# Two K loads ranked higher in a load queue, and another table of rankings, in a kernel of two attentions

## The chip, the core and the metric

The kernel runs on one core of a Trainium2 chip. A core has five engines that run their own instruction streams and meet at semaphores: TensorE (PE; matmul, with weight loads shown as PEld), VectorE (DVE), ScalarE (ACT), GpSimd (POOL) and SyncE (SP). Here SP issues all loads. Matmul results go to PSUM, eight banks of 128 x 2 KB; everything else lies in SBUF. The metric is device time in microseconds of one execution, the median of several runs.

## What is computed

Two attention blocks on different inputs; their outputs stand side by side. A has 32 query heads on 4 K/V heads (eight query heads share one), B has 32 query heads with 32 K/V heads of their own. Both have 16 batches of 32 tokens, width 1024, 1024 cached keys, heads of 128, all bf16.

```python
def _B_ref(x, k_cache, v_cache, wq, wo):
    B, Sq, D = x.shape              # 16, 32, 1024
    H, Dh = 32, 128
    q = (x @ wq).reshape(B, Sq, H, Dh).transpose(0, 2, 1, 3)
    scores = einsum("bhqd,bhkd->bhqk", q, k_cache) * (Dh ** -0.5)
    p = softmax(scores, axis=-1)
    o = einsum("bhqk,bhkd->bhqd", p, v_cache)
    return o.transpose(0, 2, 1, 3).reshape(B, Sq, H * Dh) @ wo
# _A_ref: the same with 4 heads of k_cache and v_cache, each repeated 8 times
# returned: concatenate([a, b], axis=-1)
```

B's cache is 16 x 32 x 1024 x 128 x 2 bytes for K and as much for V, 268 MB of the 338 MB that are read.

## The kernel before

**Units of work.** A is cut into 128 quads: one batch, four query heads, all 1024 keys. B is cut into 64 pairs, 0 to 63 in the program's order, each of two batches and four heads; a pair has four tiles of K (512 KB each, loaded two at a time) and four loads of V (512 KB each). For a pair of B the steps are:

- the load of K by SP (`st_dmaKB`, L904), two loads `y = 2n` and `y = 2n + 1` for pair `n`; each brings two tiles
- four transposes in place on VectorE (`st_ktrB`, L973, 128 x 1024 as f32 units)
- the scores on TensorE (`st_scoresB`, L1030, 64 small matmuls into four PSUM banks)
- two maxima on VectorE (`st_max`, L1045), the exponentials on ScalarE (`st_exp`, L1061; they free the banks), sums and exchange between lanes on GpSimd and ScalarE (`st_weights`, L1077 to L1088)
- scaling of the probabilities on GpSimd (`st_pscale`, L1161; from pair `NORM_FROM` = 61 on the outputs are scaled instead, `st_normB`, L1175 and L1176, on ScalarE or VectorE)
- two transposes on TensorE (`st_ptB`, L1132), each evacuated from PSUM (`evac`, L650), the products with V (`st_pvB`, L1149), evacuation, a small transpose (`st_otrB`, L1187), evacuation
- after every two pairs the output projection of their group of tokens (`oproj`, L817) and its addition on VectorE (L829, L838; for the very last group L833, then the store, L835)

The steps of a quad of A are alike (scores L992, maximum L1042, exponential L1054, scaling L1280, transposes L1099, products L1119, transposes of K on TensorE L966).

**Buffers.** K of B has eight tile slots in `KB_sb`, and late in the kernel four more in `wq_sb`; pair 61's K stands in slots 0 to 3 of `KB_sb`, pair 62's in slots 4 to 7, pair 63's in `wq_sb`. The V of pair 63 is loaded into slots 0 to 3 of `KB_sb` (`home_v`), once pair 61's scores have been made.

**Who sets the order.** The program is first recorded as a list of 5431 operations with their dependences, and each gets a step number. `list_schedule` then plans: it keeps a time for every engine and for the DMA stream, takes the engine that can start first, and among the operations that can start within a small look-ahead it takes the one of the highest rank. The outcome is one fixed order for each engine. On the chip each engine runs its list strictly in that order, and waits at semaphores; SP too, so a load whose slot is not free yet holds all loads behind it. An evacuation marked `any` is given to ScalarE or VectorE by the planner.

A rank is made as follows (L278). For a step before `tail_step` (120, 122 or 124) it is `bl`, the length of the path behind the operation within its step, and `step_us` (2.5 to 5) is taken off for every step number. For later steps it is the full length of the path to the end, less a base. `RANKS` holds 16 such rules. `TUNE` is a table of 71 entries: after every 77 planned operations the planner goes on to the next entry, which names the rule that holds from there. So a change of an entry changes the plan from its place on, until the two plans fall together again. The operation's own `prio` is part of `bl`, and is 0 for all here. Loads of K get a step number two or so pairs ahead of their use: loads 124 and 125, pair 62's, have step 120; loads 122 and 123, pair 61's, have 118; loads 126 and 127, pair 63's, have 122.

Of the kernel before, what the change touches and what calls it, by code (L numbers as in the profile page):

```python
# [17 lines left out]
XT_FREE = 54  # L18
LATE = 51
NORM_FROM = 61  # L20
NKB_SLOTS = 8
LAZY_PER_STEP = 100
LAZY_DELAY = 4
# [21 lines left out]
RANKS = ((3.5, 122, 0.35, 0.0, 0.3), (3.0, 122, 0.35, 0.0, 0.3), (4.0, 122, 0.35, 0.0, 0.3), (3.5, 122, 0.15, 0.0, 0.3), (2.5, 122, 0.35, 0.0, 0.3), (5.0, 122, 0.35, 0.0, 0.3),  # L45
         (3.5, 122, 0.7, 0.0, 0.3), (3.5, 120, 0.35, 0.0, 0.3), (3.0, 124, 0.2, 0.0, 0.3), (3.5, 122, 0.15, 1.5, 0.3), (3.5, 122, 0.15, -1.5, 0.3), (3.5, 122, 0.15, 0.0, 0.0),
         (3.5, 122, 0.15, 0.0, 0.7), (3.5, 122, 0.15, 4.0, 0.3), (3.5, 122, 0.15, -4.0, 0.3), (3.5, 122, 0.25, 0.0, 0.3))
TUNE = (11, 11, 6, 10, 15, 6, 8, 15, 12, 2, 7, 0, 11, 12, 9, 12, 5, 6, 0, 7, 0, 7,
        4, 4, 8, 8, 1, 1, 7, 15, 0, 7, 7, 7, 0, 0, 0, 7, 1, 2, 0, 0, 7, 0,
        3, 0, 2, 11, 15, 11, 15, 5, 3, 0, 1, 3, 6, 15, 8, 13, 3, 3, 0, 13, 10, 3,  # L50
        9, 9, 9, 3, 1)
HOLD_AHEAD = 1
STEP_NEAR = 0
TAIL_BASE = 12.0
# [76 lines left out]
class Prog:  # L131
# [118 lines left out]
    def list_schedule(self, lat=0.05, look=LOOK):  # L250
        ops = self.ops
        n = len(ops)
# [11 lines left out]
        bl = [0.0] * n  # L264
# [7 lines left out]
        full = [0.0] * n  # L272
        for i in range(n - 1, -1, -1):
            full[i] = odur(ops[i]) + max((full[u] + lat for u in users[i]), default=0.0)
        ranks = []
        for step_us, tail_step, _, bias, _ in RANKS:
            base = max((full[i] for i in range(n) if ops[i].step >= tail_step and ops[i].dma_key is None), default=0.0)
            ranks.append([(bl[i] if ops[i].step < tail_step else full[i] - base + TAIL_BASE) - step_us * min(ops[i].step, tail_step) + (bias if ops[i].first else 0.0) for i in range(n)])  # L278
        bl = ranks[0]
        ready_t = [0.0] * n  # L280
        free = {}
# [139 lines left out]
        while True:  # L421
            best = None
            bkey = None
            turn = len(order) // WINDOW
            turn = TUNE[turn] if turn < len(TUNE) else 0
            bl, look, act_first = ranks[turn], RANKS[turn][2], RANKS[turn][4]
# [70 lines left out]
        for k in seq:  # L497
            eng, emit, reads, writes, dma_key, name, dur, tag, prio = self.specs[order[k]]
# [55 lines left out]
def build(nc, pa, pb, out):  # L554
# [6 lines left out]
    Dh = pa["k"].shape[3]  # L561
    Sk = pa["k"].shape[2]
# [7 lines left out]
    NVB = NVB_SLOTS  # L570
    NKB = NKB_SLOTS
    HqA = pa["wq"].shape[1] // Dh
# [16 lines left out]
    with stack:  # L589
# [305 lines left out]
        def st_dmaKB(y):  # L895
            if y < NIT:
                kind, sl = home_k(2 * y)
                assert home_k(2 * y + 1) == (kind, sl + 1) and sl % 2 == 0
                q = quadsB[2 * (y // 2)]
                dst = (wq_sb if kind == "wq" else KB_sb)  # L900
                dst = dst[:, 2 * sl:2 * sl + 4, :].rearrange("p j c -> p (j c)") if kind == "wq" else dst[:, sl:sl + 2, :].rearrange("p i x -> p (i x)")
                src = pb["k"][q.b0 + y % 2, q.m * MS:(q.m + 1) * MS].rearrange("h (p s) d -> (h p) (s d)", s=32)
                pr.step, was = 2 * ((2 * y - NKB) // 4) if 2 * y >= NKB else pr.step, pr.step
                pr.add("sp", lambda e: e.dma_start(dst, src), writes=[(kind, sl), (kind, sl + 1)], dma_key=f"{kind.lower()}{sl}", name="kb_dma",  # L904
                       dur=4 * Sk * Dh * 2, wtag={(kind, sl): 2 * y, (kind, sl + 1): 2 * y + 1})
                pr.step = was

        V_LAST = 2 * NIT - 4
# [17 lines left out]
        def home_k(x):  # L926
            if x < XK:
                return ("KB", x % NKB)
            return ("wq", (x - XK) % (NKB + 4)) if (x - XK) % (NKB + 4) < 4 else ("KB", kb_of(x))
# [226 lines left out]
        def st_pscale(q):  # L1156
            def emit(e):
                for h_ in range(2):
                    k_ = 20 + 2 * q.e + h_
                    p_ = p2_of(q.vP)[:, h_ * 512:(h_ + 1) * 512]  # L1160
                    last = e.tensor_scalar(p_, p_, stat2[:, q.vB.idx, k_:k_ + 1], 1.0, ALU.mult, ALU.mult)  # L1161
                return last
            pr.add("pool", emit, reads=[q.vB], writes=[q.vP], name="pscaleB")

        def st_copyB(vbo, h_, vO):
            evac(lambda: O2_sb[:, vO.idx, :, :, :].rearrange("p i u d -> p (i u d)"), lambda: bank(vbo[h_]), reads=[], writes=[vbo[h_], vO], name="O_ev")
# [49 lines left out]
        def pairB(n):  # L1216
# [3 lines left out]
            if n == 0:  # L1220
                for y in range(2, NKB // 2):
                    st_dmaKB(y)
            st_scoresB(qs)
            while k_next[0] < min(NIT, 2 * n + 2 + NKB // 2 + (2 if n >= LATE else 0)):
                st_dmaKB(k_next[0])
                k_next[0] += 1
# [9 lines left out]
            for q in qs:  # L1236
                if n < NORM_FROM:
                    st_pscale(q)
# [16 lines left out]
            for h_ in range(2):  # L1255
                vO = Virt("O2")
                if n < NORM_FROM:
                    st_copyB(vbo, h_, vO)
# [36 lines left out]
        for y in range(2):  # L1295
            st_dmaKB(y)
# [122 lines left out]
```

## Time and profile before

| | us |
|---|---|
| median of 3 runs | 857.17 |
| lowest and highest | 856.28, 862.17 |
| the profiled execution | 854.25 |
| its span, first to last instruction | 852.5 |

The granted TensorE clock was 0.996 over the execution. In the profile "PE x13382" counts instructions, digits are busy tenths of a slice of 1/40 of the span (21.3 us), and a row of the order of time gives start, duration, engine, line, operation and operands; the name in brackets is what ended the idle time before it. "issue" stands for idle time without a wait that the profile shows. A DMA row with "SPq" is the time at which SP issued the load; when it landed is told by the median from issue to landing.

SP's own waits are longest for the slots of V, which products with V free (L1149), 217.0 us in 84 waits; for slots of K (freed by scores, L1030) it waits 77.3 us in 31. While SP waits the DMA engines work off what was issued before.

### The profile page before, as it was taken

What the parts mean: (1) busy time and instruction counts of PE and PEld (TensorE: products, weight loads), DVE (VectorE), ACT (ScalarE), POOL (GpSimd) and SP (SyncE); (2) the same over time, 40 slices, a digit from 0 to 9 for tenths busy, and PEclk for the clock granted to TensorE, in tenths of its full rate; (3) what the DMA queues carried; (4) which work ended last, traced back from release to release, by engine and by line L of the source; (5) the groups of instructions that cost most, each with busy time, mean ns of one, the idle gap of its engine ahead of it and who ended that gap; (6) DMA issues with size and microseconds to landing.
All of it is one profiled execution on the core that took longest, in us unless ns stands there. A gap on an engine that the chain in (4) does not pass through costs nothing.

```text
span 852.5 us, 31891 instructions
## 1 busy us (share of the span) xinstructions
PE 762.9 (89%) x13382; PEld 518.7 (61%) x13504; DVE 746.7 (88%) x960; ACT 590.9 (69%) x1458; POOL 461.9 (54%) x1160
## 2 busy tenths in 40 slices
PE   6988999989889889999998998999998898878887
PEld 5455666666566566666666656566666656555655
DVE  1598879979899888898999888899989899999986
ACT  2377777687777576777667767686677677686754
POOL 1056565646456454564655555555664645655852
PEclk9989999999999999999999999999999999999999
DMA  9999999999999999999999999999999999999993
GB/s 354 415 396 417 414 413 420 403 415 405 389 411 406 420 414 415 371 397 416 418 418 415 418 397 415 401 407 414 417 420 414 410 417 393 410 419 405 403 400 139
DMA packets 93791, 341.83 MB, mean 401 GB/s; under 512 B 10000, under 2 KB 10256, under 8 KB 77264
## 3 DMA queue, kind: packets, MB, share of 16 engines
q1 hardware_dynamic: 93088, 337.94, 98.7%
q8 instruction: 107, 1.75, 0.7%
q0 software_dynamic: 560, 1.84, 0.5%
q14 instruction: 36, 0.29, 0.1%
HBM read 337.64 MB, written 2.10 MB: 399 GB/s over the span
## 4 chain that ended last, share of the span: by engine, by line
PE 51%; DVE 21%; ACT 11%; DMA 7%; POOL 5%; issue 3%; SPq 1%; DVEq 0%; POOLq 0%; ACTq 0%
PE psum L1149 9%; PE psum L817 9%; DVE KB_sb L973 6%; DVE stat L1045 6%; PE psum L1030 6%; PE psum L1099 5%; DMA KB_sb<-in_B_k_cache_dram 5%; PE psum L1119 4%; PE psum L734 4%; ACT P_sb L1054 4%; DVE stat L1042 4%; PE psum L1132 4%; ACT P_sb L1061 4%; PE psum L774 4%; PE psum L992 3%
## 5 line engine op out<-in xcount | busy, mean ns | idle before, releaser
L973 DVE STREAM_TRANSPOSE KB_sb<-KB_sb 128x1024 f32<-128x1024 f32 x240 | 284.7, 1218 | 10.9 <-DMA KB_sb<-in_B_k_cache_dram 10.5
L1161 POOL TENSOR_SCALAR P_sb<-P_sb,stat 128x512 bf16<-128x512 bf16 x232 | 158.3, 695 | 92.7 <-DVE stat L1088 63.7
L1280 POOL TENSOR_SCALAR P_sb<-P_sb,stat 128x1024 bf16<-128x1024 bf16 x128 | 143.6, 1122 | 87.6 <-DVE stat L1196 70.1
L1077 POOL COPY stat<-stat 32x4 f32<-32x4 f32 x512 | 92.5, 181 | 173.1 <-DVE stat L1045 102.2
L1061 ACT ACTIVATE P_sb<-psum,stat 128x512 bf16<-128x512 f32 x236 | 159.4, 690 | 33.5 <-DVE stat L1045 29.1
L1054 ACT ACTIVATE P_sb<-psum,stat 128x1024 bf16<-128x1024 f32 x128 | 143.4, 1121 | 42.3 <-DVE stat L1042 41.9
L1045 DVE TENSOR_REDUCE stat<-psum 128x2 f32<-128x1024 f32 x128 | 150.2, 1211 | 23.6 <-PE psum L1030 23.0
L1042 DVE TENSOR_REDUCE stat<-psum 128x1 f32<-128x1024 f32 x128 | 153.4, 1204 | 6.6 <-PE psum L992 5.7
L650 ACT COPY PT_sb<-psum 128x512 f32<-128x512 f32 x174 | 101.5, 590 | 53.7 <-PE psum L1132 32.0
L1149 PE MATMUL psum<-VB_sb,PT_sb 64*64 64x256 bf16 x3584 | 115.2, 272 | 8.7 <-issue 2.0
L1149 PEld LDWEIGHTS psum<-VB_sb,PT_sb 64*64 64x64 bf16 x3584 | 92.4, 107 | 29.6 <-issue 21.6
L1099 PE MATMUL psum<-id,P_sb 128*128 128x128 f32 x512 | 90.3, 300 | 12.1 <-POOL P_sb L1280 3.3
L1099 PEld LDWEIGHTS psum<-id,P_sb 128*128 128x128 f32 x512 | 73.6, 208 | 33.7 <-POOL P_sb L1280 11.1
L1132 PE MATMUL psum<-id,P_sb 128*128 128x128 f32 x472 | 81.3, 300 | 11.2 <-POOL stat L1077 4.6
L1119 PE MATMUL psum<-PT_sb,VA_sb 128*128 128x128 bf16 x1024 | 79.8, 220 | 8.8 <-ACT P_sb L1054 3.6
L1132 PEld LDWEIGHTS psum<-id,P_sb 128*128 128x128 f32 x472 | 67.2, 209 | 31.3 <-POOL P_sb L1161 13.7
L1119 PEld LDWEIGHTS psum<-PT_sb,VA_sb 128*128 128x128 bf16 x1024 | 63.0, 96 | 33.9 <-issue 12.5
L1030 PE MATMUL psum<-KB_sb,QR 32*32 32x512 bf16 x3840 | 73.6, 397 | 9.0 <-ACT P_sb L1054 5.6
L650 ACT CAST O_sb<-psum 128x512 bf16<-128x512 f32 x96 | 54.2, 591 | 25.3 <-PE psum L1149 25.2
L992 PE MATMUL psum<-KTA_sb,QT_sb 128*128 128x512 bf16 x189 | 63.4, 380 | 8.1 <-ACT P_sb L1061 2.5
L817 PE MATMUL psum<-woB_sb,OTB_sb 128*128 128x512 bf16 x231 | 61.0, 379 | 6.6 <-ACT P_sb L1061 1.6
L774 PE MATMUL psum<-xT_sb,wq_sb 128*32 128x512 bf16 (+1 forms) x1024 | 64.6, 375 | 0.9 <-issue 0.9
(80 smaller groups left out, 987.9 us busy)
## 6 DMA issues: line engine op xcount, KB each, us to landing
KB_sb<-in_B_k_cache_dram SPq DMA_DIRECT2D x120, 1024.0 KB, 9.5
VB_sb<-in_B_v_cache_dram SPq DMA_DIRECT2D x234, 512.0 KB, 8.2
KA_sb<-in_A_k_cache_dram SPq DMA_DIRECT2D x64, 256.0 KB, 7.6
VA_sb<-in_A_v_cache_dram SPq DMA_DIRECT2D x64, 256.0 KB, 7.6
wq_sb<-in_B_wq_dram SPq DMA_DIRECT2D x16, 512.0 KB, 9.7
woB_sb<-in_B_wo_dram SPq DMA_DIRECT2D x32, 256.0 KB, 8.7
woA_sb<-in_A_wo_dram SPq DMA_DIRECT2D x32, 256.0 KB, 7.9
wq_sb<-in_B_k_cache_dram SPq DMA_DIRECT2D x8, 1024.0 KB, 8.4
```

What stands on the lines that cost most here:

```text
L650: return e.copy(dst, src) if hasattr(e, "activation") else e.tensor_copy(dst, src)
L973: pr.add("dve", lambda e: e.transpose(tile_k(x).bitcast(F32), tile_k(x).bitcast(F32)), writes=[home_k(x)], name="KBt_tr", rtag={home_k(x): ...
L1042: pr.add("dve", lambda e: e.tensor_reduce(stat[:, vst.idx, 0:1], both(vS), AXIS.XY, ALU.max, negate=True), writes=vS + [vst], name="max")
L1045: pr.add("dve", lambda e: e.tensor_reduce(stat2[:, q.vB.idx, 2 * q.e:2 * q.e + 2], both(vS), AXIS.X, ALU.max, negate=True), writes=vS + [q ...
L1054: return e.activation(dst, src, ACTF.Exp, bias=stat[:, vst.idx, 0:1], scale=1.0, accum_out=stat[:, vst.idx, 1:2])
L1061: last = e.activation(dst, src, ACTF.Exp, bias=stat2[:, q.vB.idx, k_:k_ + 1], scale=1.0, accum_out=stat2[:, q.vB.idx, 4 + k_:5 + k_])
L1099: last = e.transpose(bank(vb)[:, m * P:(m + 1) * P], p32[:, m:Sk // 2:NPK], id32[:])
L1119: last = e.matmul(bank(vb)[:, 0:P], VA_sb[:, kvs, c, :], ptc_of(vPT, c, 0, P), start=(c == 0), stop=(c == NCH - 1))
L1132: last = e.transpose(bank(vb)[:, m * P:(m + 1) * P], p32[:, m:Sk // 2:4], id32[:])
L1149: last = e.matmul(bank(vbo[h_])[n0:n0 + 64, i * 2 * Dh:(i + 1) * 2 * Dh], pt2_chunk(vPT, c, e0, n0), v2[e0:e0 + 64, c * 2 * Dh:(c + 1) * 2 ...
L1161: last = e.tensor_scalar(p_, p_, stat2[:, q.vB.idx, k_:k_ + 1], 1.0, ALU.mult, ALU.mult)
L1280: pr.add("pool", lambda g: g.tensor_scalar(P_sb[:, vP.idx, :], P_sb[:, vP.idx, :], stat[:, vst.idx, 2:3], 1.0, ALU.mult, ALU.mult), reads= ...
```

## The change

Two loads get a `prio` of 30 us: `KPRIO` names loads 124 and 125, both halves of the K of pair 62. The value enters `bl`, and by an added term also the rank of the late steps. 26 of the 71 entries of `TUNE` change, from the eighth on; the other 45 keep the rule that they had.

```diff
+KPRIO = {124: 30.0, 125: 30.0}
...
-TUNE = (11, 11, 6, 10, 15, 6, 8, 15, 12, 2, 7, 0, 11, 12, 9, 12, 5, 6, 0, 7, 0, 7,
-        4, 4, 8, 8, 1, 1, 7, 15, 0, 7, 7, 7, 0, 0, 0, 7, 1, 2, 0, 0, 7, 0,
-        3, 0, 2, 11, 15, 11, 15, 5, 3, 0, 1, 3, 6, 15, 8, 13, 3, 3, 0, 13, 10, 3,
-        9, 9, 9, 3, 1)
+TUNE = (11, 11, 6, 10, 15, 6, 8, 3, 12, 4, 4, 4, 11, 3, 9, 12, 5, 6, 7, 15, 0, 7,
+        4, 4, 8, 8, 1, 1, 0, 0, 0, 0, 7, 0, 0, 0, 7, 0, 0, 0, 0, 0, 7, 0,
+        0, 0, 2, 11, 15, 11, 7, 5, 3, 0, 1, 3, 6, 15, 8, 2, 2, 9, 7, 13, 12, 3,
+        14, 9, 13, 11, 9)
...
-            ranks.append([(bl[i] if ops[i].step < tail_step else full[i] - base + TAIL_BASE) - step_us * min(ops[i].step, tail_step) + ...
+            ranks.append([(bl[i] if ops[i].step < tail_step else full[i] - base + TAIL_BASE + ops[i].prio) - step_us * min(ops[i].step, tail_step) + ...
...
-                       dur=4 * Sk * Dh * 2, wtag={(kind, sl): 2 * y, (kind, sl + 1): 2 * y + 1})
+                       dur=4 * Sk * Dh * 2, prio=KPRIO.get(y, 0.0), wtag={(kind, sl): 2 * y, (kind, sl + 1): 2 * y + 1})
```

No operation is added or taken away, and no size, buffer or dependence changes. What changes is the order on each engine and the engine of some evacuations. Set beside each other, the built orders are the same up to about 125 us of the profile. They differ from there to 168 us, from 471 to 505 us, and from 707 us to the end; between these stretches every engine has the same order. On SP 76 of the 618 loads and stores stand at another place.

More of the change, by code (lines that the diff above doesn't have):

```diff
@@ L277, in list_schedule @@
             base = max((full[i] for i in range(n) if ops[i].step >= tail_step and ops[i].dma_key is None), default=0.0)
-            ranks.append([(bl[i] if ops[i].step < tail_step else full[i] - base + TAIL_BASE) - step_us * min(ops[i].step, tail_step) + (bias if ops[i].first else 0.0) for i in range(n)])
+            ranks.append([(bl[i] if ops[i].step < tail_step else full[i] - base + TAIL_BASE + ops[i].prio) - step_us * min(ops[i].step, tail_step) + (bias if ops[i].first else 0.0) for i in range(n)])
         bl = ranks[0]
```

## The prediction

> **What bounds the kernel now.** I read the page's busy shares and its DMA rows first, then a table of stretches, then the order of time of the load queue, VectorE and TensorE over the last 70 us. Pairs of the second attention are counted from 0 to 63; 63 is the last, 62 the last but one.
>
> ```profile
> span 852.5 us, 31891 instructions
> PE 762.9 (89%) x13382; PEld 518.7 (61%) x13504; DVE 746.7 (88%) x960; ACT 590.9 (69%) x1458; POOL 461.9 (54%) x1160
> DMA  9999999999999999999999999999999999999993
> HBM read 337.64 MB, written 2.10 MB: 399 GB/s over the span
> ```
>
> The DMA engines are full in 39 of 40 slices. Nothing in the change alters the bytes, so a gain has to come from the last slice or from dips in the stream. The stretches show who is full where:
>
> ```profile
> 120.00:170.00 50.00, 47.39 (x709) 31.77 (x716) 43.77 (x57) 36.00 (x89) 28.12 (x72) 1.00 1.02 413
> 470.00:510.00 40.00, 37.49 (x617) 25.01 (x623) 35.36 (x47) 30.11 (x73) 20.95 (x53) 1.00 1.01 407
> 700.00:760.00 60.00, 51.74 (x884) 36.08 (x884) 58.29 (x77) 43.67 (x102) 32.80 (x71) 1.00 1.01 406
> 760.00:800.00 40.00, 32.29 (x638) 23.08 (x644) 38.46 (x49) 30.29 (x83) 25.93 (x74) 1.00 1.02 403
> 800.00:820.00 20.00, 16.82 (x287) 12.72 (x288) 17.48 (x25) 13.12 (x31) 13.80 (x31) 1.00 1.02 418
> 820.00:835.00 15.00, 13.15 (x311) 9.38 (x311) 14.38 (x18) 8.09 (x23) 6.34 (x19) 1.00 0.98 381
> 835.00:852.50 17.50, 12.09 (x246) 8.39 (x248) 9.91 (x20) 8.49 (x28) 5.01 (x25) 1.00 0.23 87
> ```
>
> After the length of the stretch come PE, PEld, DVE, ACT and POOL busy, granted clock, DMA share and GB/s. Two things are full from 700 to 835: the DMA engines, and VectorE, which idles 1.71 + 1.54 + 2.52 + 0.62 = 6.4 us of 135. From 835 on the loads are over (share 0.23) and a chain of dependent steps runs to the end. So the end is set by when VectorE gets through the work of the last pairs, provided that their K has landed.
>
> ```profile
> 814.76 1.28 DVE L650 CAST O_sb<-psum 128x512 bf16<-128x512 f32 x2
> 817.12 0.29 DVE L650 CAST OTB_sb<-psum 128x128 bf16<-128x128 f32 x1 [1.07 <-PE psum L1187]
> ...
> 822.21 2.36 DVE L1045 TENSOR_REDUCE stat<-psum 128x2 f32<-128x1024 f32 x2 [0.56 <-PE psum L1030]
> 824.49 3.49 DVE L973 STREAM_TRANSPOSE wq_sb<-wq_sb 128x1024 f32<-128x1024 f32 x3
> 827.90 0.65 DVE L838 TENSOR_TENSOR acc<-acc,psum 128x512 bf16<-128x512 f32 x1
> 828.47 2.35 DVE L973 STREAM_TRANSPOSE KB_sb<-KB_sb 128x1024 f32<-128x1024 f32 x2
> 830.75 1.20 DVE L973 STREAM_TRANSPOSE wq_sb<-wq_sb 128x1024 f32<-128x1024 f32 x1
> 831.87 0.65 DVE L838 TENSOR_TENSOR acc<-acc,psum 128x512 bf16<-128x512 f32 x1
> 832.45 2.34 DVE L1045 TENSOR_REDUCE stat<-psum 128x2 f32<-128x1024 f32 x2
> ```
>
> From 822.21 VectorE does not rest: maxima of pair 61, three tiles of pair 63's K, two of pair 62's, one of 63's, maxima of 62. The tiles of pair 62 stand late for a reason in the load queue:
>
> ```profile
> 787.88 1.51 SPq L904 DMA_DIRECT2D KB_sb<-in_B_k_cache_dram  x2
> ...
> 798.57 0.43 SPq L904 DMA_DIRECT2D KB_sb<-in_B_k_cache_dram  x1
> ...
> 812.49 0.80 SPq L904 DMA_DIRECT2D wq_sb<-in_B_k_cache_dram  x2
> 813.33 0.43 SPq L904 DMA_DIRECT2D KB_sb<-in_B_k_cache_dram  x1
> ...
> 827.52 2.90 SPq L952 DMA_DIRECT2D KB_sb<-in_B_v_cache_dram  x4
> ```
>
> ```profile
> KB_sb<-in_B_k_cache_dram SPq DMA_DIRECT2D x1, 1024.0 KB, 10.5
> ```
>
> In order: both halves of pair 61's K, the first half of 62's, both halves of 63's, then the second half of 62's, issued at 813.33 and landed (the row of that one issue) 10.5 us later, at 823.8. It is the last K of all, and a pair that comes one earlier waits for it.
>
> **The change, part by part.** In the changed kernel's built order the 30 us lift both halves of 62's K past more than the title says: past 63's K and seven V loads, but past both halves of 61's K too. On TensorE the scores of 62 now come before those of 61; 63 stays last. VectorE has 948 instructions instead of 960, since 32 evacuations left it for ScalarE and 20 came.
>
> *The two early stretches.* The new table moves loads by one to three places at 125 to 168 and at 471 to 505 us. The same loads stay within the stretch, and DMA shares of 1.02 and 1.01 cover what shifts. I take 0; without that cover it is at most the idle share, within 1 us either way.
>
> *The last but one pair's maxima (term A).* In both orders the work ahead of the last but one pair's maxima on VectorE is the same twelve tiles of the last three pairs, the same adds and maxima; what differs is evacuations. From 717 us to there 13 large and 6 small ones leave, 7 large and 1 small come:
>
> ```profile
> L650 DVE CAST O_sb<-psum 128x512 bf16<-128x512 f32 x8 | 5.2, 684 | 0.8 <-PE psum L1149 0.7
> L650 DVE CAST OTA_sb<-psum 128x128 bf16<-128x128 f32 x4 | 1.1, 276 | 0.1
> ```
>
> 6 x 0.68 + 5 x 0.28 = 5.5 us less VectorE work. That is the upper end: it holds if VectorE waits no more than now. The lower end is TensorE. The new pair in that place, 61, has its scores behind pair 60's last products and eight output projections, as 62 has now; only 61's own transposes and the small transposes of 60's output no longer stand ahead of them:
>
> ```profile
> 825.46 1.07 PE L1149 MATMUL psum<-xT_sb,PT_sb 64*64 64x256 bf16 x32
> ...
> 828.86 1.23 PE L1132 MATMUL psum<-id,xT_sb 128*128 128x128 f32 x8
> 829.93 0.47 PE L1187 MATMUL psum<-rowsel,O_sb 128*128 128x64 bf16 x8
> 831.03 1.19 PE L1030 MATMUL psum<-KB_sb,QR 32*32 32x512 bf16 x64 [0.63 <-ACT OTB_sb L650]
> ...
> 835.19 0.91 PE L1030 MATMUL psum<-wq_sb,QR 32*32 32x512 bf16 x42 [1.10 <-ACT P_sb L1061]
> 837.61 0.65 PE L1030 MATMUL psum<-wq_sb,QR 32*32 32x512 bf16 x22 [1.50 <-issue]
> ...
> 844.27 1.94 PE L1149 MATMUL psum<-KB_sb,xT_sb 64*64 64x256 bf16 x64
> ```
>
> 1.23 + 0.47 = 1.7 us. Zero is possible too, if TensorE waits as long as now. Between 1.7 and 5.5 I take 3.0, nearer the TensorE end, because a VectorE that runs ahead early still has to wait for that queue.
>
> *A stall that moves (term B).* At 836.11 TensorE stopped in the middle of pair 63's scores for 1.50 us with nothing released ("issue"). Counted in weight loads it lies at the 13,299th of 13,504. In the new order that count falls in pair 62's products, behind 63's scores, beside ScalarE's exponentials. If the stall sits at a place in the instruction stream, up to 1.5 us leaves the chain; if it comes from something else, 0. I take 0.7.
>
> *Pair 61's leftovers (term C).* Its normalisations now come after 63's scores; two of them stand on ScalarE ahead of the last pair's two evacuations, on the chain:
>
> ```profile
> 842.70 0.86 ACT L1175 ACTIVATE O_sb<-psum,stat 128x256 bf16<-128x256 f32 x2
> ```
>
> I add 0.9 (0 to 1.5, the upper end if pair 61's sums on GpSimd, queued among 63's, hold them longer).
>
> *The last V.* The last pair's V goes where pair 61's K stood, so its four loads now wait for 61's scores, from about 830 instead of 827.52. They were used at 844.27. With the 12 us between first issue and last landing now (829.9 + 8.9 by the group's median) they land by about 842.5; without a queue ahead of them sooner. Products at 844.27 - 2.8 = 841.5 could wait up to 1 us; I take 0, since two V loads ahead of them will have drained.
>
> ```profile
> KB_sb<-in_B_v_cache_dram SPq DMA_DIRECT2D x2, 512.0 KB, 8.9
> ```
>
> Sum: -3.0 - 0.7 + 0.9 = -2.8 us. The profiled execution took 854.25 us, its span of 852.5 and 1.75 around it, so it would take 851.45. The median of the runs shown, 857.17, lies 2.9 higher; the same step from there gives 854.4.
>
> **The rivals.** *The load queue holds up (slower).* The two loads of 62's K wait for pair 59's scores; 61's K, ready at 787.88, now stands behind them.
>
> ```profile
> 791.30 1.20 PE L1030 MATMUL psum<-KB_sb,QR 32*32 32x512 bf16 x64
> ...
> 794.72 1.07 PE L1149 MATMUL psum<-VB_sb,xT_sb 64*64 64x256 bf16 x32
> 795.62 1.04 PE L1149 MATMUL psum<-xT_sb 64*64 64x256 bf16 x32
> ```
>
> In the new order 59's scores stand behind pair 57's products, which end at 796.66 here, so they end near 798 instead of 792.5, about when the first half of 62's K went out (798.57). But 2 MB that bridged this time are no longer ahead of it: at 418 GB/s, 5 us of stream. If the scores come 5 us later than 798, up to 5 us of DMA time is lost, the last K lands at 828.8 instead of 823.8, and with some 2 us of slack (its last two tiles are wanted near 826) the end is 3 us later: 857.4 by the profiled time, 860 by the median. It decides from about 2 us of lost stream. Against it: the eight projections that now precede pair 57's products may be done early. The Trainium skill, "DMA: Bandwidth & Descriptors", section "Anatomy of one DMA", states that DMA engines do not wait on semaphores, the issuing sequencer does before dispatch; that speaks for this rival, since one blocked load then blocks all behind it. No row here shows the reverse.
>
> *No change.* The stream is the bound: 337.64 + 2.10 MB end when they end, and a VectorE that is done sooner waits for the same last K at 823.8. Then A falls to its lower end or to nothing, B and C cancel: 854 by the profiled time, 857 by the median. The Trainium skill, "Perfetto Trace Analysis", section "Roofline", puts a single core's ceiling at its 16 DMA engines, about 435 GB/s; by that figure the stream would be an estimated 781 us, with room that the trace (418 at most in these stretches) does not show. Against it: VectorE reaches the last K's tiles at 828.47, 4.7 us after it landed.
>
> *More gain.* A at 5.5, B at 1.5, C at 0, and the dip to 403 GB/s between 760 and 800 filled (40 x 15 / 418 = 1.4 us): -8.4, 846 to 849.
>
> **How the numbers follow.** Forecast (1.5 to 5 us less) 0.45, no change 0.22, held queue 0.23, more gain 0.10. One per cent, what a measurement of this kernel can tell from no change, is 8.6 us. The likeliest case alone runs from 852 to 856; over the cases, 847.5 to 861.5. Faster by over 1% is the far end of the last case, 0.08; slower by over 1% needs the queue held for more than twice its price, or the median's own spread, 0.08; within, 0.84.
>
> **What would show it.** Right: the maxima of pair 61 start near 829.5 in the new profile, the two halves of 62's K are issued by 799, DMA shares stay over 1.00 to 824, no "issue" wait inside 63's scores. Wrong: a stretch near 797 to 803 with a DMA share under 0.9; VectorE idle over 4 us between 760 and 820; the last products waiting for a V load.

## The result, and the profile after

| | before | after |
|---|---|---|
| median of 18 runs each, us | 859.5 | 854.82 |
| lowest and highest, us | 856.28, 863.44 | 850.76, 860.17 |
| ratio, with its 95% interval | | 0.9955 (0.9935 to 0.9974) |
| the profiled execution, us | 854.25 | 852.65 |
| its span, us | 852.5 | 850.8 |

With more runs the median of before rose from 857.17 to 859.5. By the ratio the change takes 0.45% off, some 3.9 us (the medians alone differ by 4.7): within 1%, but by the interval not nothing. The two profiled executions differ by 1.6 us only. The page after:

```profile
span 850.8 us, 32012 instructions
PE 777.8 (91%) x13504; PEld 519.3 (61%) x13504; DVE 741.9 (87%) x948; ACT 594.1 (70%) x1470; POOL 459.9 (54%) x1160
DMA  9999999999999999999999999999999999999995
```

VectorE has 12 instructions and 4.8 us less, ScalarE 12 more. PE shows more matmuls only because fewer records are missing here. The table of stretches, same columns as in the prediction:

```profile
700.00:760.00 60.00, 53.38 (x959) 35.36 (x956) 54.90 (x70) 43.47 (x110) 36.29 (x90) 1.00 1.01 410
760.00:800.00 40.00, 35.44 (x594) 24.90 (x597) 37.24 (x46) 29.84 (x79) 23.78 (x62) 0.96 0.99 393
800.00:820.00 20.00, 17.66 (x362) 12.98 (x355) 20.00 (x27) 16.85 (x42) 14.41 (x31) 1.00 1.03 422
820.00:835.00 15.00, 13.89 (x291) 9.70 (x289) 14.39 (x16) 10.40 (x30) 6.60 (x24) 1.00 1.01 413
835.00:850.80 15.80, 11.51 (x215) 8.02 (x214) 8.08 (x20) 7.25 (x21) 3.82 (x18) 0.97 0.33 129
```

From 760 to 800 the stream is thinner than before (393 GB/s against 403), from 800 to 835 fuller (422 and 413 against 418 and 381). Next the load queue (SP), in order of time:

```profile
794.74 0.80 SPq L905 DMA_DIRECT2D KB_sb<-in_B_k_cache_dram  x2
...
802.76 1.05 SPq L905 DMA_DIRECT2D KB_sb<-in_B_k_cache_dram  x2
...
813.64 1.61 SPq L905 DMA_DIRECT2D wq_sb<-in_B_k_cache_dram  x2
...
829.87 1.85 SPq L953 DMA_DIRECT2D KB_sb<-in_B_v_cache_dram  x4
```

Both halves of pair 62's K go out at 794.74, then 61's, then 63's, then the last V. The K that comes last is now pair 63's. VectorE:

```profile
822.31 2.34 DVE L1046 TENSOR_REDUCE stat<-psum 128x2 f32<-128x1024 f32 x2
...
829.21 1.23 DVE L974 STREAM_TRANSPOSE wq_sb<-wq_sb 128x1024 f32<-128x1024 f32 x1
830.36 2.31 DVE L1046 TENSOR_REDUCE stat<-psum 128x2 f32<-128x1024 f32 x2
833.28 2.36 DVE L1046 TENSOR_REDUCE stat<-psum 128x2 f32<-128x1024 f32 x2 [0.61 <-PE psum L1031]
...
846.50 1.28 DVE L834 TENSOR_TENSOR woA_sb<-acc,psum 128x512 bf16<-128x512 f32 x2
```

These are the maxima of pairs 62, 61 and 63, and the last addition ahead of the store. TensorE:

```profile
828.62 1.20 PE L1031 MATMUL psum<-KB_sb,QR 32*32 32x512 bf16 x64
829.75 0.41 PE L1188 MATMUL psum<-rowsel,O_sb 128*128 128x64 bf16 x8
830.00 1.20 PE L1133 MATMUL psum<-id,P_sb 128*128 128x128 f32 x8
831.98 1.19 PE L1031 MATMUL psum<-wq_sb,QR 32*32 32x512 bf16 x64 [0.78 <-ACT PT_sb L651]
...
834.57 1.23 PE L1133 MATMUL psum<-id,xT_sb 128*128 128x128 f32 x8 [0.18 <-ACT xT_sb L1062]
...
836.68 1.94 PE L1150 MATMUL psum<-VB_sb,xT_sb 64*64 64x256 bf16 x64
...
840.02 0.62 PE L1150 MATMUL psum<-KB_sb,xT_sb 64*64 64x256 bf16 x14
840.86 0.73 PE L1150 MATMUL psum<-KB_sb,xT_sb 64*64 64x256 bf16 x18 [0.21 <-issue]
...
842.87 0.60 PE L818 MATMUL psum<-woB_sb,OTB_sb 128*128 128x512 bf16 x2
...
843.42 1.03 PE L818 MATMUL psum<-woB_sb,OTB_sb 128*128 128x512 bf16 x4
...
844.40 2.32 PE L818 MATMUL psum<-woB_sb,OTB_sb 128*128 128x512 bf16 x10
```

Pair 63's scores (831.98) run in one piece. In before they stopped in the middle, and had first waited 1.10 us for the exponentials (L1061) of the pair ahead of them, which free PSUM banks. By the built orders 63's scores go to banks 0, 1, 4 and 5 in before, of which pair 62, just ahead, holds 0 and 1; in after they go to 0, 1, 6 and 7, and the pair just ahead, 61, holds 2 to 5. Pair 61's transposes (834.57) and products (836.68) now stand behind 63's scores, and all sixteen output projections of the last two groups (2 + 4 + 10) behind the last products. In before ten of the sixteen stand there by the built order; fourteen have records, and nine of these (1 + 8) come behind the products of 844.27:

```profile
842.38 0.81 PE L817 MATMUL psum<-woB_sb,OTB_sb 128*128 128x512 bf16 x3
...
843.75 0.59 PE L817 MATMUL psum<-woB_sb,OTB_sb 128*128 128x512 bf16 x2
844.27 1.94 PE L1149 MATMUL psum<-KB_sb,xT_sb 64*64 64x256 bf16 x64
846.37 0.38 PE L817 MATMUL psum<-woB_sb,OTB_sb 128*128 128x512 bf16 x1 [0.16 <-issue]
...
847.48 1.90 PE L817 MATMUL psum<-woB_sb,OTB_sb 128*128 128x512 bf16 x8
848.99 1.28 DVE L833 TENSOR_TENSOR woA_sb<-acc,psum 128x512 bf16<-128x512 f32 x2 [1.06 <-PE psum L817]
```

**A landmark.** Times from the span's start are a poor measure of the last stretch: where both orders are the same, between 318 and 330 us, after falls 2.3 us behind before: TensorE stops there for 2.51 us (at 322.10, "issue"), and in before's execution it does not. The last section tells of such stops. So I count from the scores of pair 51, the last ones that stand alike in all the kernels here. The view of a line's instructions has them, in before and in after:

```profile
L1030 PE MATMUL psum<-KB_sb,QR x64: 378/394/413, 692.9 to 693.8; 32*32 32x512 bf16 x64
```

```profile
L1031 PE MATMUL psum<-KB_sb,QR x64: 371/394/417, 694.9 to 695.7; 32*32 32x512 bf16 x64
```

Five steps follow, told by their starts: **a** to the last but one pair's maxima (before 832.45 - 693.8 = 138.6), **b** on to pair 63's maxima, **c** to 63's products, **d** to the issue of the store, **e** to the end. Pair 63's maxima in before, and the store in before and in after:

```profile
838.31 2.35 DVE L1045 TENSOR_REDUCE stat<-psum 128x2 f32<-128x1024 f32 x2 [2.13 <-PE psum L1030]
...
849.77 0.87 SPq L835 DMA_DIRECT2D out_dram<-woA_sb  x2
```

```profile
847.28 0.87 SPq L836 DMA_DIRECT2D out_dram<-woA_sb  x2
```

| us | a | b | c | d | e | sum |
|---|---|---|---|---|---|---|
| before | 138.6 | 5.9 | 6.0 | 5.5 | 2.7 | 158.7 |
| after | 134.6 | 2.9 | 6.7 | 7.3 | 3.5 | 155.0 |
| difference | -4.0 | -3.0 | +0.7 | +1.8 | +0.8 | -3.7 |

The -3.7 agrees with the 3.9 of the ratio. In a and b 7.0 us were won, in c to e 3.3 given back.

### The profile page after: what moved, and what is told of

Its sections match the earlier page's. It is cut to its first block, busy times and chain, and to the rows that moved or that the text cites. A ratio compares the mean times of both kernels' runs of the same rounds, so it can differ in the third digit from the quotient of the medians.

```text
span 850.8 us, 32012 instructions
## 1 busy us (share of the span) xinstructions
PE 777.8 (91%) x13504; PEld 519.3 (61%) x13504; DVE 741.9 (87%) x948; ACT 594.1 (70%) x1470; POOL 459.9 (54%) x1160
## 4 chain that ended last, share of the span: by engine, by line
PE 51%; DVE 23%; ACT 9%; DMA 8%; POOL 6%; issue 3%; SPq 1%; DVEq 0%; POOLq 0%; ACTq 0%
PE psum L1150 9%; PE psum L818 9%; DVE stat L1046 7%; DVE KB_sb L974 7%; DMA KB_sb<-in_B_k_cache_dram 6%; PE psum L1031 6%; PE psum L1100 5%; PE psum L1120 4%; DVE stat L1043 4%; PE psum L1133 4%; PE psum L735 4%; PE psum L775 4%; ACT P_sb L1055 3%; ACT P_sb L1062 3%; PE psum L993 3%; POOL P_sb L1162 3%
## 5 line engine op out<-in xcount | busy, mean ns | idle before, releaser
L1150 PEld LDWEIGHTS psum<-VB_sb,PT_sb 64*64 64x64 bf16 x3584 | 92.3, 107 | 28.3 <-issue 19.6
L993 PE MATMUL psum<-KTA_sb,QT_sb 128*128 128x512 bf16 x256 | 82.5, 383 | 2.8 <-ACT P_sb L1062 1.6
L818 PE MATMUL psum<-woB_sb,OTB_sb 128*128 128x512 bf16 x256 | 66.5, 380 | 3.7 <-ACT P_sb L1062 1.5
L1031 PEld LDWEIGHTS psum<-KB_sb,QR 32*32 32x32 bf16 x3840 | 43.9, 88 | 35.7 <-ACT P_sb L1055 12.2
```

The costliest lines, as they stand in the source:

```text
L1031: last = e.matmul(bank(q.vS[g2])[n0:n0 + 32, :].rearrange("p (s j) -> p s j", s=16), QR[r0:r0 + 32, gp, fp, tok:tok + 32], rhs, start=(fp ...
L1150: last = e.matmul(bank(vbo[h_])[n0:n0 + 64, i * 2 * Dh:(i + 1) * 2 * Dh], pt2_chunk(vPT, c, e0, n0), v2[e0:e0 + 64, c * 2 * Dh:(c + 1) * 2 ...
```

## The experiments

The question is which part of the change brings a and b and which costs d: the table, the order of pairs 61 and 62, the evacuations that changed engine, or the load queue. All kernels compute the whole of the reference. Edits are to after; those of 5 and 7 are to before, and those of 4 and 11 to before with the two lines of code that read `KPRIO`. Times and ratios are against before on the same chip (1 to 4, 5 to 8 and 9 to 12 on one chip each); the steps are those of the table above, from one profile of each. A later table gathers them.

**1. Only the loads' rank, with the old table.**

```diff
 KPRIO = {124: 30.0, 125: 30.0}
-TUNE = (11, 11, 6, 10, 15, 6, 8, 3, 12, 4, 4, 4, 11, 3, 9, 12, 5, 6, 7, 15, 0, 7,
+TUNE = (11, 11, 6, 10, 15, 6, 8, 15, 12, 2, 7, 0, 11, 12, 9, 12, 5, 6, 0, 7, 0, 7,
...
```

> The kernel before with the two ranks of 30 and the old table: the order differs only from 789 us on, pair 62 comes before pair 61, two evacuations move to ScalarE instead of twelve. Measured for the whole change: ratio 0.9955, and 3.6 us less from the end of pair 51's scores to the end of the span (155.1 instead of 158.7). Theory 'swap': most of it comes from the swapped pairs, so 156 to 157 us from pair 51's scores, ratio 0.996 to 0.998, no stall inside pair 63's scores. Theory 'relief': it comes from the evacuations that the table moves off VectorE, so 158 to 159 us, ratio 0.999 to 1.001.

**2. Only the new table.**

```diff
-KPRIO = {124: 30.0, 125: 30.0}
+KPRIO = {}
```

> The new table without the two ranks: pair 61 stays before pair 62, and 13 evacuations leave VectorE on balance. Theory 'swap': 158 to 159 us from pair 51's scores, ratio 0.999 to 1.001, the stall inside pair 63's scores is there again. Theory 'relief': 155 to 156.5 us, ratio 0.995 to 0.997.

**3 and 4. The table cut at its 46th entry.** Experiment 3 has before's entries 0 to 45, so that the two early stretches are as in before, and after's from there on, with `KPRIO`. Experiment 4 has the reverse and an empty `KPRIO`, so only the early stretches change.

```diff
 KPRIO = {124: 30.0, 125: 30.0}
...
-        0, 0, 2, 11, 15, 11, 7, 5, 3, 0, 1, 3, 6, 15, 8, 2, 2, 9, 7, 13, 12, 3,
+        3, 0, 2, 11, 15, 11, 7, 5, 3, 0, 1, 3, 6, 15, 8, 2, 2, 9, 7, 13, 12, 3,
...
```

```diff
+KPRIO = {}
...
-        3, 0, 2, 11, 15, 11, 15, 5, 3, 0, 1, 3, 6, 15, 8, 13, 3, 3, 0, 13, 10, 3,
+        0, 0, 2, 11, 15, 11, 15, 5, 3, 0, 1, 3, 6, 15, 8, 13, 3, 3, 0, 13, 10, 3,
...
```

> The old table up to its 46th entry, the new from there, with the two ranks: every engine has the order of the kernel before up to 707 us, and that of the changed kernel behind it, but for two evacuations. Both theories put the gain here: 155 to 156 us from pair 51's scores, ratio 0.994 to 0.997. A rival, that the early stretches carry it (the profile showed 0.8 us less between pair 6's and pair 13's scores), gives 0.997 to 0.999.

> The other half: the new table up to its 46th entry, the old from there, no ranks. Up to 505 us the order of the changed kernel, from 707 us on that of the kernel before. Expected, 0 from the early stretches: ratio 0.999 to 1.001, 158 to 159.5 us from pair 51's scores. The rival: 0.997 to 0.999, with the 0.8 us less between pair 6's and pair 13's scores seen again.

**What 1 to 4 gave.** Rank alone 0.9969 (0.9938 to 1.0), table alone 1.0003 (0.9975 to 1.0032), the late part with rank 0.9944 (0.9919 to 0.9969), the early part alone 0.9994 (0.997 to 1.0017). Experiment 4 takes 92.4 us from the scores of pair 6 to those of pair 13, against 93.1 in before, as after did (92.3); the time does not show it. So the early stretches bring nothing that can be measured in the time, the new table nothing by itself, and the rank by itself 0.3 of the 0.45%, with an interval that just reaches 1. Whether the table adds to it can't be told: 0.9944 and 0.9969 lie in each other's intervals. Step a is shorter with it, 134.7 against 136.8, but c to e are longer by 1.6 us, so the sums differ by only 0.4. Experiment 2 has the natural order and yet not the stall in 63's scores that was expected there; they wait 2.81 us for exponentials instead:

```profile
838.34 1.94 PE L1031 MATMUL psum<-wq_sb,QR 32*32 32x512 bf16 x64 [2.81 <-ACT P_sb L1062]
```

**5 and 6. The order without the engines, the engines without the order.** 37 late evacuations stand on another engine in after: 24 went from VectorE to ScalarE, 13 came. Experiment 5 gives before's order after's engines for these, experiment 6 gives after's order before's engines (the two lists swapped). The lists themselves are left out here.

```diff
...
+        for i in TO_ACT:
+            chosen[i] = "act"
+        for i in TO_DVE:
+            chosen[i] = "dve"
```

> The order of the kernel before, with only the engines of the late evacuations as in the changed kernel: 24 go to ScalarE, 13 to VectorE. In the profiles of the changed kernel and of the table alone, pair 60's scores ended 115.5 to 115.7 us after pair 51's, 118.0 to 118.3 without the table. If the relief of VectorE makes that, 115.5 to 116.5 here; if the new order makes it, 118 or more. Time: 0.998 to 1.003 in both cases, since the table without the swap gave 1.0003.

> The other half: the order of the changed kernel, with the engines of the late evacuations as in the kernel before. Relief: 117.5 to 118.5 us from pair 51's scores to pair 60's, the last but one pair's maxima at 136.5 or later instead of 134.6, ratio 0.997 to 0.999. Order: 115.5 to 116.5, maxima at 134.5 to 135.5, ratio 0.994 to 0.996.

Both missed the times that were expected for them. The engines alone are slower, 1.0044 (1.0021 to 1.0068): set beside before, 1.4 us are lost between the scores of pairs 52 and 53, 3.5 by the end of pair 60's scores, 5.3 by 61's, while VectorE has less to do. After's order with before's engines gives 0.9998 (0.9977 to 1.002), with a at 140.5. So an evacuation on a less busy engine is no gain by itself. The likely reason, which no run isolates: that engine too takes its list in order, and the planner had placed the rest around its choice. Experiment 6 also shows that the swap of the pairs does not win by itself with every choice of engines: its b is as short as after's, but a and c are longer.

**7. The stall of term B.** Before, with each transpose of x at the start made twice: 64 more transposes, each with its weight load, that write the same values again and push all that follows on by 64 weight loads, or 128 instructions.

```diff
-                        for jj in range(jn):
+                        for jj in list(range(jn)) * 2:
```

> The kernel before with 64 transposes more at its start (each of the first transposes of x made twice, into the same place, with the same result), so that every later TensorE instruction stands 64 places further on in the stream; the order is untouched. If the stall of 1.5 us inside pair 63's scores belongs to a place in the stream, it moves to the end of pair 61's products: the scores take 0.9 to 1.3 us instead of 2.6, and end up to 1.3 us earlier counted from pair 51's (142.5 to 143 instead of 143.8 to 144.0). If it belongs to these instructions or to what happens beside them, 2.6 again and 144.

Pair 63's scores in this kernel, on TensorE's time line:

```profile
853.59 1.18 PE L1030 MATMUL psum<-wq_sb,QR 32*32 32x512 bf16 x64 [1.02 <-ACT P_sb L1061]
```

The stall has left them with the order of before, and b fell from 5.9 to 4.0. So the stall is not owed to the scores or to what they need, and where it falls hangs on the instruction stream ahead. By this one profile some 1.9 us of b's 3.0 are its worth, and the other 1.1 come with the order. The wait for the bank is still there (1.02). All in all the kernel is slower, 1.0073 (1.0041 to 1.0105): other stalls of the kind appeared, told in the last section. The profile is of the longest of the six executions, 871.5 us against a median of 864.46.

**8. Eight projections of A later.** After, with the last output projections of A ranked down, so that pair 61's scores need not stand behind them.

```diff
+OPROJ_PRIO = -10.0
...
-                           dur=0.45 * OUTW / 512, rtag={(wo_res, h0_): blk, (wo_res, h0_ + 1): blk, ("OTv", pi, gp): (blk, G)})
+                           dur=0.45 * OUTW / 512, prio=OPROJ_PRIO if pi == 0 and blk == nblk - 1 and G == NG - 1 else 0.0, rtag={(wo_res, h0_): blk, (wo_res, h0_ + 1): blk, ("OTv", pi, gp): (blk, G)})
```

> The changed kernel with a rank lower by 10 us for the eight last output projections of A, which stand between pair 60's products and pair 61's scores: pair 61's scores and the last tiles of K come ahead of them and of their two additions. If the TensorE queue sets the last but one pair's maxima, these start 1 to 3 us earlier than 134.6 us from pair 51's scores. If what counts from there on is how much TensorE has left to do, the end does not move: 154.5 to 156 us, ratio 0.994 to 0.997, as the 3.6 us of projections then stand behind; if the maxima set the end, 152 to 154 us and 0.991 to 0.994.

0.996 (0.9932 to 0.9988). a is 1.2 us shorter (133.4), b 1.8 longer (4.7): the projections had to be made somewhere, and came between 61's scores and 63's. This is the outcome that was expected if the work left for TensorE sets the end.

**9 to 12. Load queue and natural order.** Experiment 12 is after once more, as a mark for the others. In after the stream dips from 768 to 776 us:

```profile
768.00:772.00 4.00, 3.08 (x60) 2.73 (x52) 4.00 (x7) 3.57 (x10) 3.01 (x8) 1.00 0.87 311
772.00:776.00 4.00, 2.94 (x34) 1.30 (x47) 4.00 (x7) 1.88 (x5) 2.93 (x6) 1.00 0.82 294
```

The cause stands in SP's list and in its waits between 755 and 805:

```profile
763.00 0.43 SPq L905 DMA_DIRECT2D KB_sb<-in_B_k_cache_dram  x1
767.90 1.74 SPq L953 DMA_DIRECT2D xT_sb<-in_B_v_cache_dram  x2
```

```profile
SPq L953 <- PE psum L1150: 14.5, 4, 6.3
```

Two loads of V wait for products to free their slots, and two loads of pair 59's K, ready, stand behind. Experiment 9 puts them ahead:

```diff
...
+        for i in SOONER:
+            seq.remove(order.index(i))
+            seq.insert(seq.index(order.index(SOONER_THAN)), order.index(i))
```

Experiments 10 and 11 lift 62's K by 4 instead of 30 us, with the new and with the old table. That brings its two halves behind 61's K and ahead of 63's: the late load is mended, and the pairs keep their order. The cut is that of 10; 11 adds the line with 4.0.

```diff
-KPRIO = {124: 30.0, 125: 30.0}
+KPRIO = {124: 4.0, 125: 4.0}
```

> The changed kernel, with two loads of K for pair 59 ahead of the V loads that held up the load queue at 763 to 768 us, where the DMA share fell to 0.87 and 0.82 for 8 us (2.2 us of stream at 418 GB/s). All else in the same order. If the stream bounds the end, the dip is gone and the time falls by up to 2 us against the changed kernel: 153 to 154 us from pair 51's scores, ratio 0.992 to 0.994. If VectorE and TensorE bound it, the last K lands up to 2 us earlier (129 us instead of 130.9 from pair 51's scores) and the end stays: 154.5 to 156 us, 0.994 to 0.997.

> The changed kernel with ranks of 4 us in place of 30: the K of pair 62 comes ahead of that of pair 63 and behind that of pair 61, and the pairs stay in the order 61, 62, 63, so the second half of 62's K is no longer the last. If the gain comes from the load that was late, 155 to 156 us from pair 51's scores, ratio 0.994 to 0.997, with no leftover of pair 61 behind 63's scores. If it comes from the swap of the pairs (TensorE has pair 61's transposes and products to do while it would wait for the exponentials, and the stall leaves the scores), 158 to 160 us and 0.998 to 1.001, as with the table alone.

> The kernel before with the ranks of 4 us and the old table: only three loads of K change places, at 813 us, four tiles change places on VectorE, and one evacuation its engine. TensorE's order is that of before. Late load: 156.5 to 157.5 us, 0.996 to 0.998. Swap: 158 to 159 us, 0.999 to 1.001, and the stall inside pair 63's scores (2.6 us) is there.

> The changed kernel once more, beside the three others on the same chip. Ratio 0.994 to 0.997, 154.5 to 156.5 us from pair 51's scores, and the dip at 768 to 776 us again if it belongs to the order.

After once more (12) has the dip again, with shares of 0.88 and 0.94, so it belongs to the order. It is gone in 9:

```profile
768.00:772.00 4.00, 2.81 (x66) 2.47 (x56) 4.00 (x7) 3.39 (x8) 3.01 (x8) 1.00 1.01 420
772.00:776.00 4.00, 3.49 (x27) 1.84 (x26) 4.00 (x6) 2.34 (x6) 2.93 (x5) 1.00 1.01 418
```

That is (420 - 311 + 418 - 294) x 4 / 418 = 2.2 us of stream. The time is 0.9951 (0.9925 to 0.9978) in 9 and 0.9951 (0.9922 to 0.9981) in 12: the stream is not what sets the end, and 9 is no better version that can be told from after.

The natural order gives 1.0007 (0.9984 to 1.003) with the new table and 1.0004 (0.9979 to 1.0029) with the old one. Mending the late load alone brings nothing. With the new table its a is as short as after's (134.5). Here is what follows in it on TensorE:

```profile
838.19 1.07 PE L1150 MATMUL psum<-VB_sb,xT_sb 64*64 64x256 bf16 x32 [0.68 <-ACT xT_sb L651]
841.30 1.50 PE L1031 MATMUL psum<-wq_sb,QR 32*32 32x512 bf16 x64 [2.04 <-ACT P_sb L1062]
```

Half of pair 61's products (32 of 64) stand between the scores of 62 and of 63, and 63's scores then wait 2.04 us for 62's exponentials. By the built order all four of their banks are 62's. In after there are no products between the scores of 61 and of 63, and 63's wait 0.78 us for a copy of transposes.

**All together**, ordered by the sum (the ratio of before is 1 by definition):

| kernel | a | b | c | d | e | sum | ratio |
|---|---|---|---|---|---|---|---|
| 9, queue unblocked | 134.1 | 2.9 | 6.8 | 7.0 | 3.5 | 154.3 | 0.9951 |
| after | 134.6 | 2.9 | 6.7 | 7.3 | 3.5 | 155.0 | 0.9955 |
| 12, after again | 134.2 | 2.9 | 7.0 | 8.0 | 3.5 | 155.5 | 0.9951 |
| 8, A's projections late | 133.4 | 4.7 | 6.9 | 7.2 | 3.5 | 155.7 | 0.996 |
| 3, late part and rank | 134.7 | 2.9 | 7.2 | 8.3 | 3.1 | 156.3 | 0.9944 |
| 1, rank, old table | 136.8 | 2.9 | 6.8 | 7.1 | 3.1 | 156.7 | 0.9969 |
| 7, 64 more at the start | 138.9 | 4.0 | 6.7 | 5.5 | 2.7 | 157.7 | 1.0073 |
| before | 138.6 | 5.9 | 6.0 | 5.5 | 2.7 | 158.7 | 1 |
| 10, natural order, new table | 134.5 | 6.5 | 7.9 | 7.1 | 3.1 | 159.1 | 1.0007 |
| 4, early part | 138.4 | 6.3 | 6.7 | 5.5 | 2.7 | 159.6 | 0.9994 |
| 2, table | 137.2 | 5.0 | 7.6 | 7.1 | 3.1 | 159.9 | 1.0003 |
| 11, natural order, old table | 138.4 | 6.7 | 6.8 | 5.5 | 2.7 | 160.0 | 1.0004 |
| 6, order without engines | 140.5 | 2.9 | 8.0 | 6.8 | 3.1 | 161.3 | 0.9998 |
| 5, engines without order | 144.6 | 5.3 | 6.1 | 5.5 | 2.7 | 164.1 | 1.0044 |

Each sum less 158.7 agrees with its ratio to about 3 us (0.3%), less than the runs of one kernel differ among themselves; only 7 lost its time elsewhere. Column b splits by one thing: 2.9 wherever 61 comes behind 62, but for 8 with its projections between; 4.0 to 6.7 where it doesn't. Column d splits by another: 5.5 where the late plan is before's, 6.8 and more with the new late table or with the swap, so either part brings it. The built orders show what the two have in common: in 2 and 10 too, half of pair 61's products stand behind 62's, and all sixteen projections behind the last products, as in after.

## Why the prediction came out right, point by point

The forecast was 854.4 us and the time is 854.82; of the median that stood behind the forecast, 857.17, some 2.3 us were low, so the fairer test is the step: -2.8 forecast, -3.9 measured. The three terms that were forecast as likeliest all moved, each in the direction forecast. Two were mis-sized, in opposite directions, and both came out beyond the bounds stated for them.

- **The early stretches (0).** Right: 0.9994 for that part alone.
- **Term A (-3.0, between 0 and -5.5).** Right in size: -4.0. Of these, 2.7 are there when pair 60's scores end (118.3 us from the landmark in before, 115.6 in after, 118.2 with the old table in experiment 1), which is the part of the new table; the other 1.3 are near the 1.7 of TensorE work that no longer stands ahead, and so are the 1.8 that experiment 1, the swap with the old table, takes off a. But A alone, as experiment 10 has it without the swap, ends no sooner than before. And fewer evacuations on VectorE, the upper bound's reason, is not enough (experiment 5).
- **Term B (-0.7, between 0 and -1.5).** Mis-sized: step b shrank by 3.0. The stall left 63's scores, as hoped, and was worth 1.9 us there, more than the 1.5 of the upper bound. Part of it came back: the next place of the kind falls in the last pair's products, where TensorE stops for 0.21 us in after, 0.93 in 12 and more in 3, inside step d. What the step left out was the wait ahead of the stall, `[1.10 <-ACT P_sb L1061]` in a row that it quoted: with pair 61's products gone from between the scores, 63's no longer wait for the exponentials of the pair ahead. They start 2.7 us behind that pair's maxima in before (835.19 - 832.45) and 1.6 in after (831.98 - 830.36). These 1.1 us are what experiment 7 leaves beside the 1.9 of the stall; experiments 2 and 10 show this wait at 2.81 and 2.04 us with no stall in 63's scores (which behind it also run more slowly, 1.94 and 1.50 us against 1.19). This is what the swap brings, and it decides the sign with the new table: after against experiment 10, the same table with the natural order, is 3.6 us shorter in b.
- **Term C (+0.9, between 0 and +1.5).** Mis-sized: c, d and e together cost 3.3. It was priced by two normalisations of 0.86 us on ScalarE, but what pair 61 leaves behind is on TensorE: its transposes (1.23) and products (1.94) ahead of the last pair's products, and behind those all sixteen projections, where before had ten. The 0.8 of e go with a store of 256 KB by GpSimd, which in after is issued 0.4 us ahead of the last store (846.88) and in before 1.55 us ahead (848.22): the last store lands in a median of 2.4 us against 1.7. No run separates these shares. That B and C missed by about as much, 2.3 and 2.4 us, is luck.
- **The last V (0).** Right: issued from 829.87, a median of 8.0 us to landing, so down by about 838 to 839, and used from 840.02.
- **The rival of the held queue (0.23).** Its place was wrong: both halves of 62's K went out at 794.74, well before 799, and nothing held from 797 to 803. The same mechanism struck at 768, with a load of V in front. The Trainium skill, "DMA: Bandwidth & Descriptors", section "Anatomy of one DMA", has the issuing sequencer wait on semaphores and not the DMA engines; the trace agrees, with shares of 0.87 and 0.82 while a longest wait of 6.3 us held SP. Its 2.2 us of stream cost nothing that shows (9 against 12), so its price was wrong too: with the dip filled the last K lands 129.0 us from the landmark instead of 130.9 and 130.1 (after and 12), and a and b hardly move.
- **The rival of no change (0.22).** It needed the stream to be the bound. Experiments 9 and 12 speak against that, and VectorE shows no wait for pair 63's K in after, the last to land.
- **What would show it.** The maxima of pair 61 start at 830.36 instead of 829.5, with the execution 1.9 us late at the landmark; no "issue" wait in 63's scores; VectorE idle for 2.8 us between 760 and 820 (40 - 37.24, and 20 - 20.00), under the 4 of the condition. Wrong: DMA shares were not over 1.00 throughout (0.99 from 760 to 800).

Open stays how much the new table adds to the swap: a says some 2 us, the sum 0.4 to 1.7 (1 against 3 and after), and the intervals of the times can't tell.

## What to carry to other kernels

A wait that stands in brackets ahead of a moved step is a term of its own: ask of each which resource it is for (here a PSUM bank held until the exponentials of the pair ahead) and whether the new neighbour still holds it. When a late unit of work is put behind another, price all that it leaves behind it on every engine up to the store, and not only the queue where it was first seen. Count a last stretch from a landmark close ahead of it that is common to both kernels, since stops of some 2 us that come in one execution and not in the next lie further up.

## What the runs showed of the hardware that was not expected

TensorE stops at places in its stream for up to 3 us with nothing released ("issue"), and the places move when instructions are added far ahead. With 64 transposes more at the start, experiment 7 lost the stall in pair 63's scores and got larger ones early on; these are two of its rows, in scores and in products:

```profile
230.45 0.39 PE L1030 MATMUL psum<-KB_sb,QR 32*32 32x512 bf16 x4 [3.33 <-issue]
```

```profile
343.04 1.45 PE L1149 MATMUL psum<-VB_sb,PT_sb 64*64 64x256 bf16 x36 [2.01 <-issue]
```

From the scores of pair 13 to those of pair 34 it took 277.9 us, against 267.8 in before, though the added work is done by then; the execution profiled was the longest of the kernel's six, so this is more than is usual. The added transposes cost 0.7% in all, more than the change gains.

The size of such a stall also differs between executions of one program. In experiment 12, the same kernel as after, the last pair's products stop at the same place, after the 14th matmul, but for 0.93 us instead of 0.21:

```profile
838.52 0.62 PE L1150 MATMUL psum<-KB_sb,xT_sb 64*64 64x256 bf16 x14
840.07 0.73 PE L1150 MATMUL psum<-KB_sb,xT_sb 64*64 64x256 bf16 x18 [0.93 <-issue]
```

Where TensorE can stop, the traces do settle. Count its stream in order: each weight load, the matmul that belongs to it, and each instruction that does nothing but wait or signal. A stop is taken as a weight load that waits for no semaphore and yet starts more than 0.7 us after the one ahead of it has ended. The 14 profiles have 80 of them, and all 80 stand at the same place in a count by 256, at 192 or 193. Pair 63's scores in before stop at 27,073, which is 105 x 256 + 193. The 64 transposes of experiment 7 are 128 instructions, half of 256, and moved every such place.

An execution has about 107 of these places and stops for over 0.7 us at 3 to 9 of them, mostly where TensorE is quick: 61 of the 80 stops came when the 256 instructions ahead had been run in 5.2 us or less, which holds for only 63 of the 1405 places without a stop. The traces thus look as if instructions came in blocks of 256 and a block were sometimes late. The planner in the kernel reckons with something alike (`FETCH_BLOCK = 252`, with waiting instructions not counted, and `FETCH_US = 4.6`). What decides at a given place, and why one execution stops there and the next does not, stays open.
